# First loads on two queues, masks by half blocks, weight conversion from step 0, blocks stored after 9 steps, gates drawn from step 14: one change to an attention and two-layer expert kernel

## The chip, the core and the metric

The kernel runs on one core of one Trainium2 chip. The metric is the device time of one execution in microseconds (us). The kernel before takes 639.42 us in the median of three runs (639.33 to 639.66). The kernel computes in fp32. TensorE multiplies it as a high and a low part, so one product is three matmuls.

## The reference

B = 2, H = 8, S = 768, D = 64; `n_global` = 8, `n_local` = 96. The attention's output, 1536 tokens by 512, passes through two layers one after the other:

```python
scores = scale * q @ k.T + bias            # bias = -slope[h] * dist
keep = is_global | is_local                # first 8 keys, or the last 96 positions
a = softmax(where(keep, scores, -1e9)); x = a @ v          # -> 1536 x 512

h = (x @ w1) * (x @ w2) @ w3               # layer 1: 512 -> 1024 -> 1024
x = h @ w_out                              #          1024 -> 512
x = ((x @ w_a) * (x @ w_b)) @ w2_out       # layer 2: 512 -> 1536 -> 512
```

The inputs of the two layers' weights and the counts arrive as 64-bit words; a weight has to be converted on the chip into a high and a low fp32 part before TensorE can use it.

## The kernel before, in words

**Attention in steps.** A block is 128 queries of one batch (12 blocks); a unit is one pair of heads of a block, four units to a block, 48 units in all. The loop of `band_attention` runs over steps u. Each step puts work of several units on the engines' queues, in this order: the score matmuls of units u and u+1 on TensorE (even steps only, `sp`, L400), the exponentials of unit u-2 on ScalarE (L446), one stage of the mask generator, the transposes of unit u-5 on TensorE (`pt`, L470) with the copy out of PSUM on ScalarE (L472), the values of unit u-6 on TensorE (`pv`, L502). Then `feed` takes turns among the remaining pieces: the masked row maximum of unit u-1 on VectorE (L434), the normalisation of unit u-3 (VectorE L455, L457; GpSimd L459), the block stages that are due, and the conversion stages. Each engine runs its own queue in the order of writing, so an instruction that waits holds up everything written behind it on that engine.

**Block stages.** `block_stages` lists stage and lag in steps after the block's first unit: `store_x` copies a finished block's values into the high part `xh` (ScalarE, two instructions, L480) at lag 11, `store_x_low` subtracts for the low part `xl` (VectorE, two instructions, L486) at lag 12. Loads of keys and queries (`band_load`) have lag -6, loads of values lag 0.

**Weights.** The weights come in pieces of 512 KB (`raw`, loaded on SyncE's queue at L173). A piece passes four conversion stages, one per step: ScalarE L93 and L94 (`words`), VectorE L100, L104, L108 (`join`), ScalarE L112 (`upper`), VectorE L116 (`rest`). `feed` begins a new piece at steps 2, 5, 8 and so on, every fourth step from 20 on, and loads two pieces ahead. The result is a `w` tile.

**Gates.** After `feed`, each step draws from the generator `moe` (the "filler") while `spent` is below a budget: up to two draws of six TensorE matmuls each (`ab`, L639 to L641, 128 x 512 a matmul, or 128 x 256 for the half tiles at the start). A draw of a half tile adds 0.65 to `spent`, one of a full tile 1.3. A gate can only be drawn when its blocks are stored and its weights converted two steps before. A gate's first half tile needs the first two blocks, `xh` and `xl`. `fold` multiplies w3 and w_out on the chip, in draws of six matmuls too. `self.order` is the list in which gates and folds are drawn. When attention ends, the rest of the two layers follows without the step loop.

**The start.** `band_masks` builds the bias of each head from two numbers read from DRAM: `bias0` for a batch's first block (128 columns a head) and `bias` for the others (256 columns a head); ScalarE makes the even heads (L310), GpSimd the odd ones (L312). Keys and queries of block 0 (`kq0`) and the numbers (`ni`) are loaded on SyncE's queue at L785 and L787, before every engine reads the counts into registers (L793, L807).

Of the kernel before, what the change touches and what calls it, by code (L numbers as in the profile page):

```python
# [14 lines left out]
ALU = mybir.AluOpType  # L15

P = 128
# [14 lines left out]
class Emitter:  # L32
# [117 lines left out]
    def feed_start(self):  # L150
# [7 lines left out]
        self.order += [("gate", f, t, whole) for t in range(1, nt) for f in range(3)]  # L158
        self.order += gates(3) + folds(0, 2) + gates(4) + folds(2, 5) + gates(5) + folds(5, nf)
# [9 lines left out]
    def feed_load(self, n):  # L169
        while self.n_loaded < min(n, len(self.pieces)):  # L170
            _, src, shape = self.pieces[self.n_loaded]
            raw = self.unit("raw", shape, I32)
            self.nc.sync.dma_start(raw, src)  # L173
            self.raws.append(raw)
            self.n_loaded += 1

    def feed(self, others=(), force=False):


        turns = list(others)  # L180
        for piece in list(self.flight):
# [5 lines left out]
        if self.n_begun < len(self.pieces):  # L187
# [3 lines left out]
            pace = 3 if self.step < 20 else 4  # L191
            room = self.n_waiting < self.lead and not (self.patient and (self.step < 2 or (self.step - 2) % pace))
# [78 lines left out]
    def band_masks(self):  # L271
# [15 lines left out]

        nc.vector.tensor_scalar(out=gl[:, own], in0=gl[:, g], scalar1=self.ng, scalar2=None, op0=ALU.is_lt)
        nc.vector.tensor_scalar(out=loc, in0=rel, scalar1=0.0, scalar2=None, op0=ALU.is_ge)
        nc.vector.tensor_scalar(out=gl[:, g], in0=gl[:, own], scalar1=-far, scalar2=far, op0=ALU.mult, op1=ALU.add)  # L290
        nc.vector.scalar_tensor_tensor(out=loc, in0=rel, scalar=self.nl, in1=loc, op0=ALU.is_lt, op1=ALU.mult)
# [3 lines left out]
        nc.vector.tensor_tensor(out=near, in0=rel, in1=loc, op=ALU.mult)  # L295
        nc.vector.tensor_scalar(out=dist, in0=loc, scalar1=-far, scalar2=far, op0=ALU.mult, op1=ALU.add)
        yield

        nc.vector.tensor_scalar(out=rel[:, g], in0=loc[:, own], scalar1=-1.0, scalar2=1.0, op0=ALU.mult, op1=ALU.add)
        nc.vector.tensor_tensor(out=dist, in0=near, in1=dist, op=ALU.add)  # L300
        nc.vector.tensor_tensor(out=rel[:, g], in0=rel[:, g], in1=gl[:, g], op=ALU.mult)
        nc.vector.tensor_copy(out=dist0[:, MAX_GLOBAL:P], in_=dist[:, P + MAX_GLOBAL :])
        nc.vector.tensor_tensor(out=dist0[:, g], in0=near[:, own], in1=rel[:, g], op=ALU.add)
        nc.vector.tensor_copy(out=dist[:, g], in_=gl[:, g])


        for bias, d in ((self.bias0, dist0[:, :P]), (self.bias, dist)):
            for h in range(self.H):
                if h % 2 == 0:
                    nc.scalar.mul(bias[:, h, :], d, -self.slopes[h] / self.scale)  # L310
                else:
                    nc.gpsimd.tensor_scalar(  # L312
                        out=bias[:, h, :], in0=d, scalar1=-self.slopes[h] / self.scale, scalar2=1.0, op0=ALU.mult, op1=ALU.mult
                    )
                if h % 2 and (bias is self.bias or h == self.H - 1):
                    yield
# [192 lines left out]
    def band_attention(self, filler):  # L509
# [15 lines left out]
        next(masks)  # L525
        block_stages = (
            (C + 7, lambda t: self.store_x(t, self.pv[t])), (C + 8, lambda t: self.store_x_low(t, self.pv.pop(t))),
# [8 lines left out]
        for u in range(nu + C + 8):  # L536
# [13 lines left out]
            for _ in range(2):  # L550
                if spent < 0.7 * (u - 16):
# [224 lines left out]
def tile_kernel(ctx, tc, io):  # L776
# [7 lines left out]
    for r in range(2):  # L784
# [100 lines left out]
```

## Time and profile before

| what | us |
|---|---|
| median of three runs | 639.42 |
| the profiled execution's own time | 640.13 |
| its span in the trace | 638.3 |
| TensorE (PE) busy | 621.0 |
| VectorE (DVE) busy | 385.9 |
| ScalarE (ACT) busy | 301.0 |
| GpSimd (POOL) busy | 67.7 |

The span is the time from the first instruction to the last of the one profiled execution; its own time is measured around it and holds 1.83 us more. That execution took 0.71 us more than the median, so a time predicted for the median is the execution's own time, plus the change, less 0.71. The mean granted clock of TensorE over the span is 0.998 of full speed.

### The profile page before, as it was taken

What the parts mean: (1) busy time and instruction counts of PE and PEld (TensorE: products, weight loads), DVE (VectorE), ACT (ScalarE), POOL (GpSimd) and SP (SyncE); (2) the same over time, 40 slices, a digit from 0 to 9 for tenths busy, and PEclk for the clock granted to TensorE, in tenths of its full rate; (3) what the DMA queues carried; (4) which work ended last, traced back from release to release, by engine and by line L of the source; (5) the groups of instructions that cost most, each with busy time, mean ns of one, the idle gap of its engine ahead of it and who ended that gap; (6) DMA issues with size and microseconds to landing.
All of it is one profiled execution on the core that took longest, in us unless ns stands there. A gap on an engine that the chain in (4) does not pass through costs nothing.

```text
span 638.3 us, 8976 instructions
## 1 busy us (share of the span) xinstructions
PE 621.0 (97%) x3230; PEld 510.6 (80%) x3230; DVE 385.9 (60%) x874; ACT 301.0 (47%) x659; POOL 67.7 (11%) x118
## 2 busy tenths in 40 slices
PE   3989999999999999999999999999999999999996
PEld 3668888788888888888888888888888888888885
DVE  4888976369987576643314566556556556653343
ACT  4999887657666374723213453243243333331110
POOL 3656664300000000000000000000000000000000
PEclk9999999999999999999999999999999999999999
DMA  6999962343525142200005011111112112000004
GB/s 189 261 229 213 234 163 103 100 163 118 161 94 162 63 151 81 67 0 1 1 0 198 33 34 66 67 66 67 67 66 67 66 67 66 1 0 1 1 35 168
DMA packets 20148, 58.86 MB, mean 92 GB/s; under 512 B 2816, under 2 KB 3072, under 8 KB 20096
## 3 DMA queue, kind: packets, MB, share of 16 engines
q1 hardware_dynamic: 20096, 58.21, 31.2%
q8 instruction: 27, 0.44, 0.3%
q14 instruction: 25, 0.20, 0.1%
HBM read 55.05 MB, written 3.15 MB: 91 GB/s over the span
## 4 chain that ended last, share of the span: by engine, by line
PE 95%; ACT 1%; SPq 1%; DMA 1%; DVE 0%; issue 0%; POOL 0%; ACTq 0%; POOLq 0%
PE ab_band L639 18%; PE ab_band L641 17%; PE ab_band L640 17%; PE o_band L126 5%; PE o_band L127 5%; PE o_band L125 5%; PE pv_band L502 4%; PE y_band L127 3%; PE y_band L125 3%; PE y_band L126 3%; PE pt_band L470 3%; PE wfp_band L239 2%; PE wfp_band L237 2%; PE wfp_band L238 2%; PE sp_band L417 2%; PE sp_band L400 2%
## 5 line engine op out<-in xcount | busy, mean ns | idle before, releaser
L639 PE MATMUL ab_band<-y_band,w_band 128*128 128x512 f32 x288 | 112.0, 389 | 0.0
L640 PE MATMUL ab_band<-y_band,w_band 128*128 128x512 f32 x288 | 112.0, 389 | 0.0
L641 PE MATMUL ab_band<-y_band,w_band 128*128 128x512 f32 x288 | 112.0, 389 | 0.0
L646 ACT COPY b_band<-ab_band 128x512 f32<-128x512 f32 (+1 forms) x63 | 35.6, 567 | 157.2 <-PE ab_band L641 157.1
L639 PE MATMUL ab_band<-xh_band,w_band 128*128 128x512 f32 (+1 forms) x216 | 82.3, 381 | 0.0
L647 DVE TENSOR_TENSOR gg_band<-ab_band,b_band 128x512 f32<-128x512 f32 x36 | 24.9, 691 | 92.0 <-ACT b_band L646 92.0
L640 PE MATMUL ab_band<-xl_band,w_band 128*128 128x512 f32 (+1 forms) x216 | 79.0, 366 | 0.0
L641 PE MATMUL ab_band<-xh_band,w_band 128*128 128x512 f32 (+1 forms) x216 | 78.9, 365 | 0.0
L112 ACT CAST w_band<-g_band 128x512 fp32r<-128x512 f32 x76 | 47.3, 623 | 48.2 <-DVE g_band L108 47.2
L639 PEld LDWEIGHTS ab_band<-y_band,w_band 128*128 128x128 f32 x288 | 54.1, 188 | 11.3
L640 PEld LDWEIGHTS ab_band<-y_band,w_band 128*128 128x128 f32 x288 | 54.1, 188 | 11.2
L641 PEld LDWEIGHTS ab_band<-y_band,w_band 128*128 128x128 f32 x288 | 54.1, 188 | 11.1
L459 POOL TENSOR_SCALAR s_band<-s_band,z_band 128x256 f32<-128x256 f32 (+1 forms) x96 | 57.9, 616 | 42.9 <-DVE z_band L457 22.9
L108 DVE CUSTOM_DVE_ANT_0 g_band<-raw_band,g_band 128x1024 uint16<-128x1024 uint16 x76 | 53.0, 697 | 10.8 <-DVE g_band L104 0.5
L126 PE MATMUL o_band<-w_band,g_band 128*128 128x512 f32 (+1 forms) x146 | 56.4, 386 | 0.0
L127 PE MATMUL o_band<-w_band,g_band 128*128 128x512 f32 (+1 forms) x146 | 56.4, 386 | 0.0
L125 PE MATMUL o_band<-w_band,g_band 128*128 128x512 f32 (+1 forms) x146 | 56.4, 386 | 0.0
L104 DVE SCALAR_TENSOR_TENSOR g_band<-raw_band,g_band 128x512 int32<-128x512 int32 x76 | 52.5, 690 | 2.3
L116 DVE TENSOR_TENSOR w_band<-g_band,w_band 128x512 fp32r<-128x512 f32 x76 | 50.9, 686 | 2.9 <-ACT w_band L112 2.3
L93 ACT ACTIVATE g_band<-raw_band 128x512 f32<-128x512 f32 x76 | 50.8, 668 | 1.3 <-DMA raw_band<-in_moe_w_dram 1.3
L94 ACT ACTIVATE raw_band<-raw_band 128x512 int32<-128x512 uint32 x76 | 50.7, 666 | 0.0
L639 PEld LDWEIGHTS ab_band<-xh_band,w_band 128*128 128x128 f32 x216 | 40.5, 188 | 11.5 <-issue 4.6
(92 smaller groups left out, 1042.6 us busy)
## 6 DMA issues: line engine op xcount, KB each, us to landing
raw_band<-in_moe_w_dram SPq DMA_DIRECT2D x32, 512.0 KB, 4.0
raw_band<-in_moe_w_out_dram SPq DMA_DIRECT2D x20, 512.0 KB, 4.3
raw_band<-in_moe_w_a_dram SPq DMA_DIRECT2D x12, 512.0 KB, 3.7
raw_band<-in_moe_w_b_dram SPq DMA_DIRECT2D x12, 512.0 KB, 3.9
v_band<-in_v_dram SPq DMA_DIRECT2D x12, 256.0 KB, 7.7
kd_band<-in_kq_dram SPq DMA_DIRECT2D x12, 256.0 KB, 8.9
qd_band<-in_kq_dram SPq DMA_DIRECT2D x12, 256.0 KB, 9.1
out_dram<-acc_band SPq DMA_DIRECT2D x11, 256.0 KB, 2.0
```

Source lines behind the costliest of these rows:

```text
L93: nc.scalar.activation(out=g, in_=f32(high), func=AF.Copy, scale=WORD_SCALE)
L94: nc.scalar.activation(out=low, in_=low.bitcast(U32), func=AF.Copy, scale=2.0**-29)
L104: nc.vector.scalar_tensor_tensor(out=gi, in0=high, scalar=-0x80000000, in1=gi, op0=ALU.bitwise_and, op1=ALU.bitwise_or)
L108: nc.vector.tensor_tensor(out=gi, in0=gi, in1=low, op=ALU.add)
L116: nc.vector.tensor_tensor(out=lo, in0=g, in1=f32(hi), op=ALU.subtract)
L125: self.nc.tensor.matmul(out, wl, xh, start=(i == 0), stop=False)
L126: self.nc.tensor.matmul(out, wh, xl, start=False, stop=False)
L127: self.nc.tensor.matmul(out, wh, xh, start=False, stop=(i == n - 1))
L459: nc.gpsimd.tensor_scalar(out=s[:, j, lo:], in0=s[:, j, lo:], scalar1=z[:, j : j + 1], scalar2=1.0, op0=ALU.mult, op1=ALU.mult)
L639: nc.tensor.matmul(p, wl, xh, start=(c == 0), stop=False)
L640: nc.tensor.matmul(p, wh, xl, start=False, stop=False)
L641: nc.tensor.matmul(p, wh, xh, start=False, stop=(c == self.C - 1))
```

## The change

It does seven things, all in the attention phase and what prepares it. (1) The numbers, the second half of `kq0` and the first two raw weight pieces are loaded on ScalarE's queue; SyncE keeps the first half of `kq0`. (2) `band_masks` works on the upper 128 columns first, makes `bias0` from them in the same stage (ScalarE heads 0, 1, 4, 5; GpSimd the others), then the lower 128 columns, and the even heads of `bias` on VectorE. (3) Keys and queries of a block come in two DMAs of 256 KB in place of four of 128 KB. (4) Pieces are begun at steps 0, 2, 5, 8 and so on; in steps below 6 all attention turns of VectorE are written ahead of the conversion turns. (5) Blocks are stored two steps sooner (lags 9 and 10), and the loop is two steps shorter. (6) The budget is 0.85 (u - 13), less 0.15 for each step over 38, in place of 0.7 (u - 16), so draws begin at step 14 in place of 17. (7) In the list of draws the gates of f = 3 move ahead to the first group, and folds 2 to 7 come in one run after the gates of f = 5.

```diff
-        self.order += [("gate", f, t, whole) for t in range(1, nt) for f in range(3)]
-        self.order += gates(3) + folds(0, 2) + gates(4) + folds(2, 5) + gates(5) + folds(5, nf)
+        self.order += [("gate", 3, 0, whole)]
+        self.order += [("gate", f, t, whole) for t in range(1, nt) for f in range(4)]
+        self.order += gates(4) + folds(0, 2) + gates(5) + folds(2, 5) + folds(5, nf)
...
+        if self.patient and self.step < 6:
+            while turns:
+                for turn in list(turns):
+                    if next(turn, turns) is turns:
+                        turns.remove(turn)
...
-            pace = 3 if self.step < 20 else 4
-            room = self.n_waiting < self.lead and not (self.patient and (self.step < 2 or (self.step - 2) % pace))
+            due = self.step in (0, 2) or (self.step > 4 and (self.step - 2) % (3 if self.step < 20 else 4) == 0)
+            room = self.n_waiting < self.lead and (due or not self.patient)
...
+        local(slice(P, W))
+        first = dist0[:, own]
...
+            if h % 4 < 2:
+                nc.scalar.mul(self.bias0[:, h, :], dist0[:, :P], factor)
+            else:
+                nc.gpsimd.tensor_scalar(
...
+        local(slice(0, P))
...
+            engine = nc.vector if h % 2 == 0 else nc.gpsimd
+            engine.tensor_scalar(
+                out=self.bias[:, h, :], in0=dist, scalar1=factor, scalar2=1.0, op0=ALU.mult, op1=ALU.mult
+            )
...
-                for n in range(2):
-                    self.load_rows(self.kq[t][:, n], t, n)
+                for r in range(2):
+                    nc.sync.dma_start(
+                        self.kq[t][r * D : (r + 1) * D], self.io["kq"][b, i, :, :, r * self.C : (r + 1) * self.C]
+                    )
...
+        self.feed_load(self.ahead, self.nc.scalar)
         self.band_load(1)
-        self.feed_load(self.ahead)
...
-            (C + 7, lambda t: self.store_x(t, self.pv[t])), (C + 8, lambda t: self.store_x_low(t, self.pv.pop(t))),
+            (C + 5, lambda t: self.store_x(t, self.pv[t])), (C + 6, lambda t: self.store_x_low(t, self.pv.pop(t))),
...
-        for u in range(nu + C + 8):
+        for u in range(nu + C + 6):
...
-                if spent < 0.7 * (u - 16):
+                if spent < 0.85 * (u - 13) - 0.15 * max(u - 38, 0):
...
-    for r in range(2):
-        nc.sync.dma_start(kq0[r * D : (r + 1) * D], io["kq"][0, 0, :, :, r * H // 2 : (r + 1) * H // 2])
...
-        nc.sync.dma_start(ni, io["n"].unsqueeze(0).broadcast_to([P, 4]))
+        nc.scalar.dma_start(ni, io["n"].unsqueeze(0).broadcast_to([P, 4]))
+    for r, queue in enumerate((nc.sync, nc.scalar)):
+        queue.dma_start(kq0[r * D : (r + 1) * D], io["kq"][0, 0, :, :, r * H // 2 : (r + 1) * H // 2])
```

ScalarE (ACT), the start of its program before: the eight bias instructions, in between the exponentials of unit 0 (`s_band_276`), then the words of piece 0 (`raw_band_233`), the exponentials of units 1 to 3.

```order
L310 ACTIVATE bias_band_225<-dist_band_222 128x128 x4
L310 ACTIVATE bias_band_224<-dist_band_221 128x256 x2
L446 ACTIVATE s_band_276,z_band_286<-s_band_276,m_band_277 128x128 x2
L310 ACTIVATE bias_band_224<-dist_band_221 128x256
L93 ACTIVATE g_band_297<-raw_band_233 128x512
L94 ACTIVATE raw_band_233<-raw_band_233 128x512
L446 ACTIVATE s_band_300,z_band_306<-s_band_300,m_band_301 128x128 x2
L310 ACTIVATE bias_band_224<-dist_band_221 128x256
L446 ACTIVATE s_band_312,z_band_333<-s_band_312,m_band_313 128x128 x2
L112 CAST w_band_296<-g_band_297 128x512
L446 ACTIVATE s_band_340,z_band_349<-s_band_340,m_band_341 128x128 x2
L472 COPY pt_band_355<-pt_band_352 128x2x128
```

The same place of the changed kernel:

```order
L175 DMA raw_band_228<-in_moe_w_dram 128x1024
L175 DMA raw_band_230<-in_moe_w_dram 128x1024
L323 ACTIVATE bias_band_225<-dist_band_222 128x128 x4
L93 ACTIVATE g_band_277<-raw_band_228 128x512
L94 ACTIVATE raw_band_228<-raw_band_228 128x512
L471 ACTIVATE s_band_284,z_band_297<-s_band_284,m_band_285 128x128 x2
L112 CAST w_band_276<-g_band_277 128x512
L93 ACTIVATE g_band_310<-raw_band_230 128x512
L94 ACTIVATE raw_band_230<-raw_band_230 128x512
L471 ACTIVATE s_band_305,z_band_316<-s_band_305,m_band_306 128x128 x2
L471 ACTIVATE s_band_322,z_band_344<-s_band_322,m_band_323 128x128 x2
L112 CAST w_band_309<-g_band_310 128x512
```

The two raw loads stand on ScalarE's queue now, the even heads' `bias` is gone from it, and L93 and L94 of piece 0 stand ahead of the exponentials of unit 0, those of piece 1 ahead of unit 1.

TensorE (PE) before, around the first gate: the transposes of unit 11 and the values of unit 10 (step 16, rows 1 and 2), the transposes of unit 12 and the values of unit 11 (step 17, rows 3 and 4), then the first gate's half tile (`ab_band_772`). A name stands as out<-operands.

```order
L470 MATMUL pt_band_716<-ident,s_band_594 128x128 x4
L502 MATMUL pv_band_650<-pt_band_683,v_band_449 64x128 x4
L470 MATMUL pt_band_745<-ident,s_band_621 128x128 x4
L502 MATMUL pv_band_650<-pt_band_721,v_band_449 64x128 x4
L639 MATMUL ab_band_772<-xh_band_544,w_band_296 128x256
L640 MATMUL ab_band_772<-xl_band_545,w_band_296 128x256
L641 MATMUL ab_band_772<-xh_band_544,w_band_296 128x256
L639 MATMUL ab_band_772<-xh_band_544,w_band_296 128x256
```

The same place of the changed kernel, at step 14 (transposes of unit 9, values of unit 8, then the first gate):

```order
L495 MATMUL pt_band_652<-ident,s_band_534 128x128 x4
L527 MATMUL pv_band_659<-pt_band_622,v_band_458 64x128 x4
L663 MATMUL ab_band_685<-xh_band_489,w_band_276 128x256
L664 MATMUL ab_band_685<-xl_band_490,w_band_276 128x256
L665 MATMUL ab_band_685<-xh_band_489,w_band_276 128x256
L663 MATMUL ab_band_685<-xh_band_489,w_band_276 128x256
L664 MATMUL ab_band_685<-xl_band_490,w_band_276 128x256
L665 MATMUL ab_band_685<-xh_band_489,w_band_276 128x256
L663 MATMUL ab_band_685<-xh_band_491,w_band_276 128x256
L664 MATMUL ab_band_685<-xl_band_492,w_band_276 128x256
```

The gate's first six matmuls read `xh_band_489` and `xl_band_490` (heads 0 to 3 of the first two blocks), the next six `xh_band_491` and `xl_band_492` (heads 4 to 7).

VectorE (DVE) before, where block 1 is stored (step 16), one step ahead of the first gate: L434 is the maximum, L455 and L457 the normalisation, L486 the low part.

```order
L434 ISA s_band_731,m_band_732<-sp_band_631,bias_band_224 128x256
L434 ISA m_band_732 128x1
L455 TENSOR_SCALAR z_band_675<-z_band_675 128x2
L486 TENSOR_TENSOR xl_band_545<-pv_band_511,xh_band_544 128x2x128
L434 ISA s_band_731,m_band_732<-sp_band_631,bias_band_224 128x256
L434 ISA m_band_732 128x1
L457 RECIPROCAL z_band_675<-z_band_675 128x2
L486 TENSOR_TENSOR xl_band_547<-pv_band_511,xh_band_546 128x2x128
```

The same place of the changed kernel (step 14, the step of the first gate):

```order
L459 ISA s_band_671,m_band_672<-sp_band_576,bias_band_224 128x256
L459 ISA m_band_672 128x1
L480 TENSOR_SCALAR z_band_614<-z_band_614 128x2
L511 TENSOR_TENSOR xl_band_490<-pv_band_526,xh_band_489 128x2x128
L116 TENSOR_TENSOR w_band_560<-g_band_561,w_band_560 128x512
L459 ISA s_band_671,m_band_672<-sp_band_576,bias_band_224 128x256
L459 ISA m_band_672 128x1
L482 RECIPROCAL z_band_614<-z_band_614 128x2
L511 TENSOR_TENSOR xl_band_492<-pv_band_526,xh_band_491 128x2x128
```

The first low part stands behind one maximum as before; between the two there is now also the last conversion stage (L116) of the fifth piece, and all of it stands in the step in which the first gate is drawn.

## Rows read from the trace of the kernel before

**Rows 1.** The page: TensorE's busy time; the chain that ended last, by engine.
```profile
PE 621.0 (97%) x3230; PEld 510.6 (80%) x3230; DVE 385.9 (60%) x874; ACT 301.0 (47%) x659; POOL 67.7 (11%) x118
...
PE 95%; ACT 1%; SPq 1%; DMA 1%; DVE 0%; issue 0%; POOL 0%; ACTq 0%; POOLq 0%
```

**Rows 2.** Windows: us, then PE, PEld, DVE, ACT, POOL busy, clock, DMA, GB/s.
```profile
10.00:20.00 10.00, 6.93 (x42) 4.79 (x40) 6.97 (x34) 8.75 (x33) 6.14 (x13) 1.00 1.04 306
41.70:638.30 596.60, 591.53 (x2982) 489.02 (x2978) 355.87 (x732) 268.97 (x558) 46.06 (x75) 1.00 0.28 83
```

**Rows 3.** Waits of TensorE: total us, times, longest us.
```profile
PE pv_band L502 <- ACT pt_band L472: 2.6, 3, 1.6
```

**Rows 4.** Chain of waits in the first 43 us: start, us, what.
```profile
2.74 1.34 SPq L793
...
5.41 0.51 SPq L327
...
7.87 4.81 DMA raw_band<-in_moe_w_dram
...
16.30 2.01 PE sp_band L400 x16
...
25.18 1.09 PE sp_band L400 x16
```

**Rows 5.** Timeline of TensorE around the first gate: start, us, what.
```profile
35.41 0.67 PE L502 MATMUL pv_band<-pt_band,v_band 128*64 128x128 f32 x8
36.01 0.66 PE L470 MATMUL pt_band<-ident,s_band 128*128 128x128 f32 x4
36.59 0.66 PE L502 MATMUL pv_band<-pt_band,v_band 128*64 128x128 f32 x8
...
41.78 0.39 PE L639 MATMUL ab_band<-xh_band,w_band 128*128 128x256 f32 x1
...
43.39 0.49 PE L400 MATMUL sp_band<-kq_band,kq_band 64*128 64x128 f32 x4
```

**Rows 6.** Timeline of SyncE's DMA issues, first row.
```profile
0.74 1.32 SPq L785 DMA_DIRECT2D kq<-in_kq_dram  x2
```

**Rows 7.** DMA issues in the first 14 us: last number, us to landing.
```profile
kq<-in_kq_dram SPq DMA_DIRECT2D x2, 256.0 KB, 3.9
```

**Rows 8.** All raw loads of the first 30 us: issue to landing.
```profile
DMA to landing us min/median/max: 4.8/6.9/7.7
```

**Rows 9.** Timeline of ScalarE, 12 to 20 us.
```profile
12.71 0.66 ACT L93 ACTIVATE g_band<-raw_band 128x512 f32<-128x512 f32 x1 [1.25 <-DMA raw_band<-in_moe_w_dram]
...
13.83 0.39 ACT L446 ACTIVATE s_band<-s_band,m_band 128x128 f32<-128x128 f32 x1
...
14.60 0.40 ACT L310 ACTIVATE bias_band<-dist_band 128x256 bf16<-128x256 f32 x1
...
17.21 0.67 ACT L93 ACTIVATE g_band<-raw_band 128x512 f32<-128x512 f32 x1
...
18.34 0.49 ACT L446 ACTIVATE s_band<-s_band,m_band 128x256 f32<-128x256 f32 x1
```

**Rows 10.** Timeline of ScalarE, 26 to 37 us.
```profile
27.84 0.62 ACT L112 CAST w_band<-g_band 128x512 fp32r<-128x512 f32 x1
28.36 0.51 ACT L446 ACTIVATE s_band<-s_band,m_band 128x256 f32<-128x256 f32 x1
...
29.36 0.57 ACT L472 COPY pt_band<-pt_band 128x512 f32<-128x512 f32 x1
29.82 0.64 ACT L480 CAST xh_band<-pv_band 128x256 fp32r<-128x256 f32 x2
30.35 0.72 ACT L93 ACTIVATE g_band<-raw_band 128x512 f32<-128x512 f32 x1
```

**Rows 11.** Timeline of VectorE, 30 to 39.5 us.
```profile
35.10 0.69 DVE L116 TENSOR_TENSOR w_band<-g_band,w_band 128x512 fp32r<-128x512 f32 x1 [0.16 <-ACT w_band L112]
35.71 0.41 DVE L434 CUSTOM_DVE_ANT_0 s_band<-sp_band,bias_band 128x256 f32<-128x256 f32 x1
```

More of the change, by code (lines that the diff above doesn't have):

```diff
@@ L167, in feed_start, with feed_load @@
         self.place = {key: i for i, (key, _) in enumerate(self.jobs)}
-    def feed_load(self, n):
+    def feed_load(self, n, queue=None):
+        queue = queue or self.nc.sync
         while self.n_loaded < min(n, len(self.pieces)):
@@ L172, in feed_load @@
             raw = self.unit("raw", shape, I32)
-            self.nc.sync.dma_start(raw, src)
+            queue.dma_start(raw, src)
             self.raws.append(raw)
@@ L294, in band_masks @@
         )
-        nc.vector.tensor_tensor(out=near, in0=rel, in1=loc, op=ALU.mult)
-        nc.vector.tensor_scalar(out=dist, in0=loc, scalar1=-far, scalar2=far, op0=ALU.mult, op1=ALU.add)
+        local(slice(P, W))
+        first = dist0[:, own]
+        nc.vector.tensor_scalar(out=first, in0=loc[:, own], scalar1=-1.0, scalar2=1.0, op0=ALU.mult, op1=ALU.add)
+        nc.vector.tensor_tensor(out=dist0[:, :P], in0=near[:, P:], in1=dist[:, P:], op=ALU.add)
+        nc.vector.tensor_tensor(out=first, in0=first, in1=gl[:, g], op=ALU.mult)
@@ L297, in band_masks @@
+        nc.vector.tensor_tensor(out=dist0[:, g], in0=near[:, own], in1=first, op=ALU.add)
+        for h in range(self.H):
+            factor = -self.slopes[h] / self.scale
+            if h % 4 < 2:
+                nc.scalar.mul(self.bias0[:, h, :], dist0[:, :P], factor)
+            else:
+                nc.gpsimd.tensor_scalar(
+                    out=self.bias0[:, h, :], in0=dist0[:, :P], scalar1=factor, scalar2=1.0, op0=ALU.mult, op1=ALU.mult
+                )
         yield
-        nc.vector.tensor_scalar(out=rel[:, g], in0=loc[:, own], scalar1=-1.0, scalar2=1.0, op0=ALU.mult, op1=ALU.add)
+        local(slice(0, P))
@@ L300, in band_masks @@
         nc.vector.tensor_tensor(out=dist, in0=near, in1=dist, op=ALU.add)
-        nc.vector.tensor_tensor(out=rel[:, g], in0=rel[:, g], in1=gl[:, g], op=ALU.mult)
-        nc.vector.tensor_copy(out=dist0[:, MAX_GLOBAL:P], in_=dist[:, P + MAX_GLOBAL :])
-        nc.vector.tensor_tensor(out=dist0[:, g], in0=near[:, own], in1=rel[:, g], op=ALU.add)
         nc.vector.tensor_copy(out=dist[:, g], in_=gl[:, g])
[L307 to L316, printed above, removed]
+        for h in range(self.H):
+            factor = -self.slopes[h] / self.scale
+            engine = nc.vector if h % 2 == 0 else nc.gpsimd
+            engine.tensor_scalar(
+                out=self.bias[:, h, :], in0=dist, scalar1=factor, scalar2=1.0, op0=ALU.mult, op1=ALU.mult
+            )
+            if h % 2:
+                yield
@@ L334, in band_load @@
                 self.kq[t] = self.unit("kq", [P, 2, self.C, P])
[L335 to L336 removed]
+                for r in range(2):
+                    nc.sync.dma_start(
+                        self.kq[t][r * D : (r + 1) * D], self.io["kq"][b, i, :, :, r * self.C : (r + 1) * self.C]
+                    )
         else:
```

9 lines of the change are left out of this document (6 added, 3 removed).

## The prediction, as it was made before the changed kernel ran

> **What bounds the kernel now.** I read the page first, then windows, then the waits and the start of the chain, then single engines there. TensorE is busy for 621.0 of 638.3 us and holds 95% of the chain [rows 1]; the reader should look for the few microseconds in which it isn't. They lie in the first 42: from 41.70 to the end it is busy for 591.53 of 596.60 us, at full granted clock, while VectorE and ScalarE have two fifths and more of that stretch free [rows 2]. So the end is the moment at which TensorE becomes continuous, plus the work that is then left. That moment is the first gate, at 41.78 [rows 5]: before it TensorE still waits for the copies of transposes on ScalarE, 2.6 us in three waits [rows 3]. And what sets the pace up to there is ScalarE, which waits for the first raw piece (1.25 us, until 12.71) and then runs without a break, words, exponentials and copies in one queue [rows 9, 10].
>
> The chain shows why the first piece comes then [rows 4]: SyncE issues the loads of block 0, reads the counts (from 2.74), issues the next block's loads from 5.41 on, and the raw piece at 7.87; that lands 4.81 us later.
>
> **The change, term by term.** I make the sum for the moment at which TensorE becomes continuous.
>
> *A. Gates from step 14.* The gates' slot of step 14 opens when the values of unit 8 end, at 36.01 [rows 5]. Before, 5.77 us pass from there to the first gate. In them lie three transposes (0.58 each, 36.01 to 36.59), three values (0.60 each, 35.41 to 36.01) and one set of scores (1.09, [rows 4]), together 4.63. That work isn't saved, it only comes behind the gates. The rest, 5.77 - 4.63 = 1.14, is waiting that the gates now fill. **Gain 1.1.**
>
> *B. The whole front comes sooner.* New head: the words of piece 0 stand in front of the exponentials of unit 0 on ScalarE, so everything there begins when the first raw piece lands. Its DMA is the third on ScalarE's queue. Two issues take 0.74 to 2.06 on SyncE [rows 6]; reading the counts took SyncE 5.41 - 2.74 = 2.67 [rows 4]; so it goes out at about 4.7 in place of 7.87. For its flight the trace gives 3.9 us for 256 KB at the very start [rows 7] and 4.8 to 7.7 for raw pieces, median 6.9 [rows 8]. The first of its queue and only just behind block 0, it is nearest to the two low rows: 8.6 to 9.5, I take **9.0**; the far bound is 4.7 + 7.7 = 12.4. I cost the masks at nothing: before, ScalarE was through with unit 0's and stood idle 1.25 us for the piece [rows 9], and now less mask work stands ahead of it on VectorE and ScalarE, and the numbers are the first load of a queue. If they are late all the same, it is unit 0's exponentials that wait, and these stand behind the words, whose 1.13 us cover as much.
>
> From there to the exponentials of unit 12 ScalarE has, in its new order: five pairs of words at 1.13 (17.21 to 18.34), four exponential pairs of 128 columns at 0.77 (13.83 to 14.60) [rows 9]; five high parts (L112) at 0.52, eight pairs of 256 columns at 1.00, five copies of 512 at 0.46, four copies of 256 at half of that, two stores at 0.53 [rows 10]. That is 5.65 + 3.08 + 2.60 + 8.00 + 2.30 + 0.92 + 1.06 = 23.6 us. To it come waits: behind the words stand the three joining passes on VectorE before L112 can run, and only one exponential pair fills them for pieces 0 and 1, an estimate of 0.9 each from the VectorE passes of 0.6 to 0.7 (the row of L116 is one of them [rows 11]), and 0.3 for a store that waits for its values. So exponentials of unit 12 start at 9.0 + 23.6 + 2.1 = 34.7. The values of unit 8 need the copy of unit 8, which stands ahead of one store (0.53) and one high part (0.52): it ends at 33.7, and the values, which began at 35.41 before, begin there. **Gain 1.7.** The slot of step 14 opens at 34.3.
>
> *C. A new wait in that slot.* The first gate's second half reads the second low part of block 1. VectorE makes it in the same step, behind the conversion's last stage (L116), a maximum and a reciprocal. L116 waits for L112, which ends as unit 12's exponentials start (34.7), plus 0.16; it takes 0.61 (35.10 to 35.71), the maximum 0.4 and the low part, of the same 128 x 256, about 0.4 [rows 11]. That is 36.3. The first half of the gate is done at 34.3 + 0.8 (twelve such matmuls took 41.78 to 43.39 [rows 5]), so TensorE waits 1.2 in front of the second. Queued behind are all its attention steps. **Loss 1.2.** Bounds: nothing, if VectorE has those passes done by then, or 2, if the maximum waits too.
>
> *At nothing:* larger key loads, the lower columns of the masks, one more conversion and the even heads' bias on VectorE (its share of that early stretch is 6.97 of 10 us [rows 2]), gates of f = 3 ahead of the folds (the same matmuls in another order; weights convert in time as long as VectorE keeps the room that it shows there, 355.87 of 596.60), and the shorter loop.
>
> Sum: 1.1 + 1.7 - 1.2 = 1.6 us sooner. The profiled execution took 640.13 for its span of 638.3, which is 0.71 above the median; so the time is 638.5 by that execution and **637.8** by the median.
>
> **Rivals.** The scale first: 0.2% is 1.3 us, about what a measurement of this kernel can tell from no change.
>
> *No difference: the raw piece shares the engines.* The sum hangs on the landing: each microsecond later than 9.0 is a microsecond less. Beside the raw piece go the second raw piece and block 1's keys and queries, 512 KB each. At the 306 GB/s of the saturated stretch [rows 2] these 1.5 MB take 5.1 us, and if all three end together the piece lands at 4.7 + 5.1 = 9.8 at best and, with the 0.7 that the first two issues took on SyncE each [rows 6] as a start, at 10.5: then the gain is 0.1 and the time **639.3**. For it: the DMA engines stand at 1.04 of their share there. Against it: the first raw piece took 4.81 while another raw piece and the keys flew beside it. The Trainium skill ("DMA: Bandwidth & Descriptors", section "Issuing engines are not separate DMA queues") says that DMAs started by different engines run on the same 16 engines and interleave, so that a second issuing engine only saves the time of issuing. By that rule this rival is the whole of the second queue's effect: 3.2 us of issue, and no faster flight. The trace of before, with one issuing engine, cannot show it.
>
> *Slower: the raw piece takes as long as the longest before.* 7.7 us [rows 8] from 4.7 is 12.4; the front is then 1.7 us later than with no gain at all, and A less C gives nothing back: **641.2**. It decides from a landing at about 11.9 on, where the sum is -1.3. For it: SyncE sends block 1's keys, values and a third raw piece in the same stretch, which it did later before. Against it: the raw loads with the long flights were issued later, behind full queues; this one has none ahead of it.
>
> *Faster still: no new wait.* If VectorE runs ahead of ScalarE in step 14, C is nothing and the time **636.6**. Against it: L116 can't run before L112, which stands directly ahead of the exponentials of unit 12.
>
> *TensorE stays at its lower rate longer.* The same 16 score matmuls take 2.01 us at 16.30 and 1.09 at 25.18 [rows 4]: by that TensorE ran at the lower of its levels (1.2 of 2.4 GHz) up to some point between, though the windows print a granted clock of 1.00 there [rows 2]; it had waited for much of the time before. If the front comes 3 us sooner but with more holes, the lower rate may last as long as before; since ScalarE sets the pace there, I give that 0.3 us and no chance of its own.
>
> **How the numbers follow.** My forecast (landing up to 9.3, or later with a smaller wait) has 0.40, no new wait 0.12, sharing within 0.2% 0.33, slower 0.15. Faster by over 0.2% takes the first two, 0.52. The range runs from 635.5 (landing at 8.6, no wait, and a microsecond of the lower rate gained) to 640.4, a landing at 11.6, near the end of the sharing case; what lies outside is most of the slower case and the far end of the best.
>
> **What would show it.** First L93 at 9.0; exponentials of unit 12 at 34.7; first gate at 34.3, then a wait of about 1.2 us for VectorE's L511 in front of an L664; no wait of TensorE for ScalarE's copies after 37. Wrong would be: L93 later than 10.5; TensorE waiting after the first gate for copies or weights, which would mean that ScalarE or the conversions still set the pace with the steeper budget; or waits for weights at the folds that now stand in one run.

## The result, and the profile after

The changed kernel takes 645.05 us in the median of four runs (643.51 to 645.95) against 639.38: a ratio of 1.0079 with a 95% interval of 1.0066 to 1.0092. The medians differ by 5.7 us, the ratio corresponds to 5.1 (4.2 to 5.9): it is slower, where 1.6 us less had been forecast. Its profiled execution has a span of 643.4 us, 5.1 more than before.

The page of the changed kernel: busy times, and the granted clock in 40 slices (tenths of full speed). The first line answers to [rows 1].

```profile
PE 622.1 (97%) x3230; PEld 510.7 (79%) x3230; DVE 387.8 (60%) x882; ACT 301.4 (47%) x655; POOL 69.2 (11%) x118
...
PEclk9999998999999999999999999999999999999999
```

TensorE's work is nearly the same (622.1 us busy against 621.0), so the 5.1 us are time in which it waits, or runs at a lower rate: one slice of the clock, the seventh, from 97 to 113 us, stands at 8 tenths. The waits of TensorE in the changed kernel (total us, times, longest us):

```profile
PE sp_band L425 <- DMA kq<-in_kq_dram: 5.8, 2, 5.6
...
PE pv_band L527 <- ACT pt_band L497: 2.4, 3, 1.1
PE ab_band L664 <- DVE xl_band L511: 1.8, 1, 1.8
PE pt_band L495 <- POOL s_band L484: 1.0, 1, 1.0
PE pt_band L495 <- ACT g_band L93: 0.5, 1, 0.5
```

The first two lines belong to the start, before the first gate. The last three are new, and all lie behind 70 us. Where they cost is seen in windows of the changed kernel (columns as in [rows 2]):

```profile
42.00:70.00 28.00, 28.00 (x274) 23.67 (x274) 23.34 (x84) 24.49 (x72) 14.77 (x20) 1.00 0.94 216
70.00:95.00 25.00, 23.48 (x181) 18.87 (x180) 20.95 (x82) 19.20 (x62) 15.70 (x23) 1.00 0.70 180
95.00:112.00 17.00, 15.15 (x109) 11.59 (x107) 9.32 (x35) 11.50 (x31) 6.96 (x12) 0.90 0.11 29
112.00:140.00 28.00, 27.86 (x214) 21.65 (x213) 12.49 (x61) 17.50 (x54) 10.24 (x20) 1.00 0.40 129
105.00:110.00 5.00, 5.00 (x34) 3.91 (x33) 1.33 (x9) 2.66 (x7) 2.86 (x5) 0.70 0.00 0
```

and in one of the kernel before:

```profile
70.00:112.00 42.00, 41.82 (x352) 34.70 (x348) 31.33 (x130) 32.66 (x103) 22.74 (x38) 1.00 0.62 157
```

Up to 70 us nothing is lost. Between 70 and 112 TensorE is not busy for 1.52 + 1.85 = 3.37 us (0.18 before), and from 105 to 110 its granted clock is 0.70. What the low clock costs is seen in two equal groups of eight score matmuls in the chain of the changed kernel, 0.95 us at 94 and 1.81 at 107:

```profile
94.21 0.95 PE sp_band L442 x8
...
106.59 1.81 PE sp_band L442 x8
```

The start, on the other hand, came nearly as forecast. TensorE around the first gate, to be read against [rows 5]:

```profile
32.47 0.67 PE L527 MATMUL pv_band<-pt_band,v_band 128*64 128x128 f32 x8 [1.08 <-ACT pt_band L497]
...
34.16 0.66 PE L495 MATMUL pt_band<-ident,s_band 128*128 128x128 f32 x4
34.74 0.67 PE L527 MATMUL pv_band<-pt_band,v_band 128*64 128x128 f32 x8
35.34 0.39 PE L663 MATMUL ab_band<-xh_band,w_band 128*128 128x256 f32 x1
...
36.16 0.28 PE L663 MATMUL ab_band<-xh_band,w_band 128*128 128x256 f32 x1
36.46 0.39 PE L664 MATMUL ab_band<-xl_band,w_band 128*128 128x256 f32 x1
```

ScalarE at the first words and at the exponentials of unit 12:

```profile
8.60 0.66 ACT L93 ACTIVATE g_band<-raw_band 128x512 f32<-128x512 f32 x1 [0.43 <-DMA raw_band<-in_moe_w_dram]
...
34.78 0.57 ACT L471 ACTIVATE s_band<-s_band,m_band 128x256 f32<-128x256 f32 x1
```

The first words run at 8.60 (forecast 9.0), the exponentials of unit 12 at 34.78 (34.7), the first gate at 35.34 (34.3), with 0.3 us lost in it between 36.16 and 36.46 (1.2). The first gate is 6.44 us sooner than before; 4.63 of these are work that moved behind it, 0.2 to 0.3 the new wait, so at 42 us the kernel is 1.5 to 1.6 us ahead. It then loses 6.6.

Why TensorE waits is read on VectorE. Its timeline in the changed kernel (L671 is the product that ends a gate, L395 and L398 the low parts of the next block's keys and queries, L511 the low part of a stored block):

```profile
75.97 0.43 DVE L671 TENSOR_TENSOR g_band<-ab_band,b_band 128x256 f32<-128x256 f32 x1 [2.74 <-ACT b_band L670]
...
76.85 1.22 DVE L395 TENSOR_TENSOR ks_band<-kd_band,ks_band 64x1024 fp32r<-64x1024 f32 x1
...
79.13 1.21 DVE L398 TENSOR_TENSOR qb_band<-qd_band,qa_band 128x1024 fp32r<-128x1024 f32 x1
...
98.43 0.69 DVE L671 TENSOR_TENSOR g_band<-ab_band,b_band 128x512 f32<-128x512 f32 x1 [4.35 <-ACT b_band L670]
...
99.58 1.22 DVE L395 TENSOR_TENSOR ks_band<-kd_band,ks_band 64x1024 fp32r<-64x1024 f32 x1
...
101.26 1.21 DVE L398 TENSOR_TENSOR qb_band<-qd_band,qa_band 128x1024 fp32r<-128x1024 f32 x1
...
102.79 0.42 DVE L511 TENSOR_TENSOR xl_band<-pv_band,xh_band 128x256 fp32r<-128x256 f32 x1
```

Twice VectorE stands at a gate's product, 2.74 us up to 75.97 and 4.35 us up to 98.43, because TensorE has not finished that gate and ScalarE has not copied it (L670). Behind it, after one maximum, come L395 and L398 with 1.2 us each, and what TensorE needs next stands behind those: at 103 the first gate of the second tile waits for the low part that L511 writes at 102.79.

```profile
103.27 0.50 PE L664 MATMUL ab_band<-xl_band,w_band 128*128 128x512 f32 x1 [1.84 <-DVE xl_band L511]
```

### The profile page after: what moved, and what is told of

The parts are those of the page before. It is cut to its first block, busy times and chain, and to the rows that moved or that the text cites. A ratio compares the mean times of both kernels' runs of the same rounds, so it can differ in the third digit from the quotient of the medians.

```text
span 643.4 us, 8956 instructions
## 1 busy us (share of the span) xinstructions
PE 622.1 (97%) x3230; PEld 510.7 (79%) x3230; DVE 387.8 (60%) x882; ACT 301.4 (47%) x655; POOL 69.2 (11%) x118
## 4 chain that ended last, share of the span: by engine, by line
PE 92%; DVE 3%; ACT 3%; issue 1%; DVEq 0%; POOL 0%; ACTq 0%; POOLq 0%
PE ab_band L663 18%; PE ab_band L664 17%; PE ab_band L665 17%; PE o_band L127 5%; PE o_band L125 5%; PE o_band L126 5%; PE y_band L126 3%; PE y_band L125 3%; PE y_band L127 3%; PE pv_band L527 3%; PE pt_band L495 3%; PE wfp_band L246 2%; PE wfp_band L245 2%; PE wfp_band L247 2%; PE sp_band L442 2%
## 5 line engine op out<-in xcount | busy, mean ns | idle before, releaser
L670 ACT COPY b_band<-ab_band 128x512 f32<-128x512 f32 (+1 forms) x63 | 35.6, 567 | 155.9 <-PE ab_band L665 155.8
L671 DVE TENSOR_TENSOR gg_band<-ab_band,b_band 128x512 f32<-128x512 f32 x36 | 24.9, 691 | 92.2 <-ACT b_band L670 92.2
L484 POOL TENSOR_SCALAR s_band<-s_band,z_band 128x256 f32<-128x256 f32 (+1 forms) x96 | 58.9, 624 | 56.1 <-DVE z_band L482 39.2
L116 DVE TENSOR_TENSOR w_band<-g_band,w_band 128x512 fp32r<-128x512 f32 x76 | 52.4, 705 | 3.0 <-ACT w_band L112 2.4
L93 ACT ACTIVATE g_band<-raw_band 128x512 f32<-128x512 f32 x76 | 51.0, 671 | 0.4 <-DMA raw_band<-in_moe_w_dram 0.4
L94 ACT ACTIVATE raw_band<-raw_band 128x512 int32<-128x512 uint32 x76 | 51.1, 673 | 0.0
```

The source lines that it names most:

```text
L93: nc.scalar.activation(out=g, in_=f32(high), func=AF.Copy, scale=WORD_SCALE)
L94: nc.scalar.activation(out=low, in_=low.bitcast(U32), func=AF.Copy, scale=2.0**-29)
L116: nc.vector.tensor_tensor(out=lo, in0=g, in1=f32(hi), op=ALU.subtract)
L484: nc.gpsimd.tensor_scalar(out=s[:, j, lo:], in0=s[:, j, lo:], scalar1=z[:, j : j + 1], scalar2=1.0, op0=ALU.mult, op1=ALU.mult)
```

## The experiments

All times are medians; the ratio is to runs of the kernel before on the same chip (639.4 to 639.8 there); "idle" is the time in which TensorE is not busy from 70 to 112 us of the profiled execution.

| run | us | ratio to before, 95% interval | idle, us |
|---|---|---|---|
| changed kernel | 645.05 | 1.0066 to 1.0092 | 3.37 |
| e1 start alone | 640.37 | 1.0000 to 1.0022 | 0.18 |
| e2 flatter budget | 642.98 | 1.0028 to 1.0057 | 1.16 |
| e3 gates held one step | 644.77 | 1.0069 to 1.0099 | 3.39 |
| e4 all products later | 641.11 | 1.0015 to 1.0035 | 0.88 |
| e5 split one step sooner | 639.11 | 0.9984 to 1.0003 | 0.00 |
| e6 old store lags | 643.42 | 1.0038 to 1.0064 | 1.15 |
| e7 old order of gates | 641.98 | 1.0022 to 1.0042 | 0.96 |
| e8 e4 and e5 | 640.13 | 0.9992 to 1.0016 | 0.27 |
| e9 two products later | 641.16 | 1.0012 to 1.0030 | 0.85 |
| e10 all but these two | 645.68 | 1.0081 to 1.0112 | 3.31 |
| e11 e5, keys first | 639.94 | 1.0002 to 1.0033 | 0.00 |
| e12 e8, keys first | 640.10 | 1.0000 to 1.0019 | 0.14 |
| e13 draws alone | 644.65 | 1.0066 to 1.0104 | 3.95 |
| e14 e5 without the start | 639.54 | 0.9992 to 1.0018 | 0.10 |

### e1: the start alone

```diff
-                if spent < 0.85 * (u - 13) - 0.15 * max(u - 38, 0):
+                if spent < 0.7 * (u - 16):
```
with the store lags, the loop and the order of gates of before.

> The new start alone (first loads on two queues, masks by half blocks, conversion from step 0) with the budget, the order of gates and the store lags of before. Theory M (the loss is made after 70 us by the drawing of gates, and the start gains 1.5): first L93 at about 8.6, no TensorE wait between 70 and 130 us, granted clock 1.00 there, time 637.5 to 638.2. Rival F (the start is at fault, since earlier conversions fill VectorE later on): TensorE waits of some us after 70 us and a time of 642 or more.

Theory M was right on the place (no new wait behind 70 us), wrong on the time: 640.37, no gain. In its profile:

```profile
32.43 0.89 PE L526 MATMUL pv_band<-pt_band,v_band 128*64 128x128 f32 x8 [1.62 <-ACT pt_band L496]
33.25 0.80 PE L424 MATMUL sp_band<-kq_band,kq_band 64*128 64x128 f32 x4
...
42.25 0.38 PE L662 MATMUL ab_band<-xh_band,w_band 128*128 128x256 f32 x1
```

TensorE waits 1.62 us for the copy of unit 7 and runs the next scores at the lower rate (0.80 for the first four, 0.49 at the full one), and its first gate is at 42.25, no sooner than the 41.78 of before [rows 5].

### e2, e3: a flatter budget, and gates held one step

```diff
-                if spent < 0.85 * (u - 13) - 0.15 * max(u - 38, 0):
+                if spent < 0.7 * (u - 13):
```

> The changed kernel with a budget of 0.7 (u - 13): draws still begin at step 14, but gates of the second tile are reached at step 43 in place of 38. Theory M: the wait of 1.84 us for the low part at 103 us and the lower clock behind it are gone, VectorE keeps up, 638 to 639. Rival F: still 642 or more. Rival O (the order of gates or the earlier storing is at fault, at any slope): waits of TensorE for VectorE's results around 80 to 105 us stay, 641 or more.

```diff
-            while self.stored * P < tg * TG + at.stop or ...
+            while self.stored * P < tg * TG + at.stop or (self.patient and tg and self.step <= self.stored_at) or ...
```

> The changed kernel, but a gate of the second or third tile is drawn at the earliest one step after its last block was stored. Theory M1 (the loss is mostly the one wait for the low part in step 38, 1.84 us, and the lower clock behind it, 1.9 us): that wait is gone, granted clock 1.00 around 105 us, time 641 to 641.5. Rival M2 (VectorE itself is late there, the wait only moves to the next thing that it makes): 643.5 to 645 as before.

e3 lets a gate of the second or third tile be drawn at the earliest one step after its last block was stored (the dots stand for the rest of the line). The flatter budget takes away 2.1 us of the 5.7, so a steep budget is not all of it; with the gates held, the wait for the low part is gone, but TensorE waits 1.9 us at one set of transposes for L484 instead, and the time stays. The second is what M2 said: VectorE is late, and whatever it makes next is waited for.

### e4: the product of a gate one draw later

```diff
-                if c % 2 and not (w is pair[-1] and c == self.C - 1):
+                if c % 2 and (self.patient or not (w is pair[-1] and c == self.C - 1)):
                     yield 1.3 * (at.stop - at.start) / TG
             ps.append(p)
...
-            yield 1.3 * (at.stop - at.start) / TG
+            if not self.deferred:
+                yield 1.3 * (at.stop - at.start) / TG
```

The draw now ends ahead of the copy and the product, and these are written at the start of the next draw.

> The changed kernel with the copy and the product of a finished gate written one draw later, behind the maxima of the next step, so that VectorE does not stand at the product while TensorE still works at that gate. Theory Q (VectorE's waits in its queue, 2.74 us at 76 and 4.35 us at 98, make its block work late, and TensorE waits for it): these waits shrink below 1 us, the waits of TensorE at 80, 91 and 103 us too, 638.5 to 640.5. Rival: VectorE is simply short of time there, 643 to 645; or the gate's banks come free later and TensorE waits for them, over 645.

641.11: 3.9 us of the loss are gone with the same matmuls in the same order, a little less than theory Q said. So TensorE's waits come from VectorE's waits in its own queue.

### e5 to e7: which part of the change brings it

e5 moves the split, and with it the loads, of the second batch's blocks:

```diff
-            (0, self.band_load_v), (C - 1, self.band_global), (-3, self.band_low), (-4, self.band_high), (-6, self.band_load),
+            (0, self.band_load_v), (C - 1, self.band_global), (-4, self.band_low), (-5, self.band_high),
+            (-8, lambda t: None if self.whole(t) else self.band_load(t)), (-6, lambda t: self.band_load(t) if self.whole(t) else None),
```

> The changed kernel with the split of keys and queries (high and low part) one step sooner for the second batch's blocks, at lags -5 and -4 in place of -4 and -3, and their loads at lag -8. With the stores of before the two heavy VectorE stages of a block fell in steps 0 and 1 of every four, light steps behind; with the earlier stores they fall in steps 1 and 2, ahead of the conversion's joining passes in step 3. Theory L (this bunching makes VectorE late, and TensorE waits for maxima and normalised rows at 80 to 105 us): the stages fall in steps 0 and 2 now, the waits for L484 and for the low part shrink by half or more, 640 to 642. Rival Q (only the standing at a gate's product matters): 643.5 to 645.5.

e6 undoes the earlier storing:

```diff
-            (C + 5, lambda t: self.store_x(t, self.pv[t])), (C + 6, lambda t: self.store_x_low(t, self.pv.pop(t))),
+            (C + 7, lambda t: self.store_x(t, self.pv[t])), (C + 8, lambda t: self.store_x_low(t, self.pv.pop(t))),
...
-                if spent < 0.85 * (u - 13) - 0.15 * max(u - 38, 0):
+                if spent < 0.85 * (u - 16) - 0.15 * max(u - 41, 0):
```

> The changed kernel with the store lags of before (11 and 12), and the same budget slope and order three steps later (draws from step 17). Theory L (the earlier storing is what makes VectorE late): no waits of TensorE for L484 between 60 and 110 us, 639 to 640.5. Rival S (the steep budget makes the gates catch up with storing): the waits stay, in particular a wait for the low part at the first gate of the second tile, drawn at step 41, one step behind its storing; 642 to 645.

e7 takes the budget of e2 and the `self.order` of before:

> The changed kernel with the order of gates of before and a budget of 0.7 (u - 13): the first tile has three gates, done at step 35, and steps 36 and 37 draw nothing, since the second tile's blocks are not stored. Beside the run with the same budget and the new order (643.0) it shows the order alone. If the order is at fault: 640 to 641. If the earlier storing is at fault: 643 or, with the two empty steps, up to 645.

e5 gives the whole loss back, more than either theory said: 639.11, TensorE never idle from 70 to 112 us.

```profile
70.00:112.00 42.00, 42.00 (x335) 34.11 (x334) 35.72 (x135) 34.95 (x106) 26.42 (x40) 1.00 0.51 135
```

But e6 speaks against theory L as I had put it: with the old lags the loss stays at 4 us. Nor is it rival S, whose wait for the low part at step 41 did not occur. e7, at 641.98 between its two cases, shows that the order alone isn't it either. What e6 shares with the changed kernel is seen on its VectorE:

```profile
74.53 0.42 DVE L671 TENSOR_TENSOR g_band<-ab_band,b_band 128x256 f32<-128x256 f32 x1 [2.54 <-ACT b_band L670]
...
75.41 1.22 DVE L395 TENSOR_TENSOR ks_band<-kd_band,ks_band 64x1024 fp32r<-64x1024 f32 x1
```

It stands 2.54 us at a product, and the split of keys (L395) follows. TensorE's idle time there is 1.15 us in e6, so this is only a part of its 4 us. In the program the split is written in steps 21, 25, 29 and so on (lag -3), and the gates end, in the changed kernel, in steps 16, 19, 22, 25, 28, 31 and 36; in e6 in 19, 22, 25, 28, 31, 34, 39; before, in 19, 23, 27, 30, 34, 38. A gate that ends in a step divisible by four has its product right ahead of the split; the changed kernel has two of them among the split steps (28 and 36), e6 one (28), the kernel before none. By the same count e2 and e7 have two early ones (20 and 24): in e2 VectorE stands at these products for 2.21 us at 54.13 and 1.61 at 64.49, with L395 at 55.00 and 65.23, and TensorE waits 0.69 us at 69. In e5 the split stands ahead of such a product, and VectorE works through it while TensorE still multiplies; at the first of the two products (L672) there is no wait any more, and at the second, at 97.22, it is 1.58 us, with the split already done:

```profile
73.78 1.34 DVE L395 TENSOR_TENSOR ks_band<-kd_band,ks_band 64x1024 fp32r<-64x1024 f32 x1
...
75.44 1.21 DVE L398 TENSOR_TENSOR qb_band<-qd_band,qa_band 128x1024 fp32r<-128x1024 f32 x1
76.74 0.42 DVE L672 TENSOR_TENSOR g_band<-ab_band,b_band 128x256 f32<-128x256 f32 x1
```

e5 moves the loads of keys too. That these come sooner is not what helps: among ScalarE's waits in the changed kernel from 42 to 128 us there is none for a load.

### e8: both cures

The edits of e4 and e5 together.

> Both cures together: the product of a gate written one draw later, and the split of keys and queries one step sooner. If standing at the product (Q) and bunching (L) are two causes, this takes away both: no wait of TensorE over 0.5 us behind 42 us, and the 1.6 us that the changed kernel is ahead at 42 us are kept: 637.5 to 639. If they are one cause, 641 as with the deferred product alone.

640.13: nothing beyond e5. Waits of TensorE over 0.5 us behind 42 us are gone, as said, but in its profiled execution TensorE reached the full rate late (four score matmuls take 0.80 us at 21.19 and 26.11, as in e9 in the last section), and the time is no better.

### e9, e10: the two products, and all the others

```diff
+    def late_product(self):
+        return self.patient and self.step in (28, 36)      # e10: not in
...
-                if c % 2 and not (w is pair[-1] and c == self.C - 1):
+                last = w is pair[-1] and c == self.C - 1
+                if c % 2 and (not last or self.late_product()):
+                    late = last
                     yield 1.3 * (at.stop - at.start) / TG
```

> The changed kernel with the copy and product written one draw later for two gates alone, those that end in steps 28 and 36. Theory P (it is the phase: a gate that ends in a step divisible by four makes VectorE stand at its product directly ahead of the step that splits the next block's keys and queries, 2.4 us of VectorE, so that the wait cannot be made up): these two products are the whole effect, the waits of TensorE at 80, 91 and 103 us go, 640 to 641.5, as with all products deferred. Rival Q (every wait at a product adds up): little is gained, 643 to 645.

> The opposite: all products of the attention phase one draw later, except those of the two gates that end in steps 28 and 36. Theory P: the waits at 80, 91 and 103 us stay, 643.5 to 645.5. Rival Q: most of the gain of the run with all products deferred, 641 to 642.5.

This pair, on one chip, decides it. VectorE's longest group of waits from 70 to 110 us, none of them at a product, and TensorE's window in e9:

```profile
DVE ks_band L395 <- ACT ks_band L383: 4.5, 3, 1.8
```

```profile
70.00:112.00 42.00, 41.15 (x327) 33.13 (x328) 36.09 (x137) 35.11 (x108) 25.53 (x39) 1.00 0.48 127
```

and in e10, where the group at the product (L677) is back:

```profile
DVE g_band L677 <- ACT b_band L676: 8.6, 4, 4.4
```

```profile
70.00:112.00 42.00, 38.69 (x282) 30.62 (x282) 29.39 (x116) 30.11 (x91) 20.57 (x33) 0.96 0.43 111
```

Two products of 0.4 and 0.7 us, written one draw later, take the time from 645.05 to 641.16, the same as all of them together (641.11). All the others written later, and these two left, give 645.68. Rival Q falls also by the sum of VectorE's waits at products from 42 to 128 us, here in the changed kernel and in the kernel before:

```profile
DVE g_band L671 <- ACT b_band L670: 15.9, 6, 4.3
```

```profile
DVE g_band L647 <- ACT b_band L646: 10.7, 7, 3.7
```

The kernel before stands at products for 10.7 us, and its TensorE is idle for 0.18 us from 70 to 112; the VectorE of e2, 2.1 us faster than the changed kernel, stands there for 12.2. Of the two theories P is left: it matters what stands behind the waiting product.

### e11, e12: keys ahead of the second piece

```diff
-        self.feed_load(self.ahead, self.nc.scalar)
+        self.feed_load(1, self.nc.scalar)
         self.band_load(1)
+        self.feed_load(self.ahead)
```

> The version with the split of keys and queries one step sooner, and only the first raw piece on ScalarE's queue, the second on SyncE's behind block 1's keys and queries. If these land sooner by the second raw piece's share (1 to 2 us before 13.3), TensorE begins the second scores at about 11.5 and reaches its full rate sooner: up to 1.2 us less than with the split alone, 638 to 639. If the second piece's words come late by it, no gain: 639 to 640.

> The same with every product of the attention phase one draw later. If the 0.6 us waits that are left at gates' ends (at 55 and 69 us) are worth taking away: 637.5 to 638.5; if the later writing itself costs what it saves: 638.5 to 640.

Neither gains: 639.94 and 640.10, though the keys do land sooner: the last wait of the second scores for them ends at 11.49 in e11, at 13.30 in the changed kernel.

```profile
11.49 0.58 PE L425 MATMUL sp_band<-kq,kq_band 64*128 64x128 f32 x1 [1.01 <-DMA kq_band<-in_kq_dram]
```

```profile
13.30 0.58 PE L425 MATMUL sp_band<-kq,kq_band 64*128 64x128 f32 x1 [2.17 <-DMA kq_band<-in_kq_dram]
```

The profiled execution of e12 has the shortest span of all profiled ones, 637.4, but the times of e12 go from 639.05 to 642.26, and no interval lies below 1. I found no version that beats the kernel before beyond its interval; e5 is nearest.

### e13, e14: the draws without the start

The kernel before with the lags, the budget and the order of the changed one (e13), and with the edit of e5 besides (e14).

> The kernel before with only the draws of the changed one: stores at lags 9 and 10, budget from step 14, the new order of gates; loads, masks and the first conversions as before. Theory: the start is worth little, since the values of unit 8 were held by TensorE's own work and not by ScalarE's copy, and the two waits ahead of blocks' splitting come from the draws alone: waits for L459 or for the low part at about 80 and 103 us as in the changed kernel, 643 to 645.5. Rival: the start is worth 1.7 us, so without it 646 to 647.

> The same with keys and queries split one step sooner. Theory: no long wait is left behind 42 us, and the start of before serves as well as the new one: 638.5 to 639.8. Rival: without the new start 1 to 1.7 us more than with it (639.1 measured there), 640 to 641.

644.65 and 639.54: with and without the new start the same, in either company (645.05 and 639.11). The draws alone make the loss, with the same waits of TensorE, here from 42 to 140 us of e13:

```profile
PE ab_band L641 <- DVE xl_band L487: 2.4, 1, 2.4
PE pt_band L471 <- POOL s_band L460: 1.0, 1, 1.0
```

## Why the prediction was wrong

**The step that failed** is the premise of the sum, "the end is the moment at which TensorE becomes continuous, plus the work that is then left", and with it the last item, "at nothing", which left VectorE out because it "keeps the room that it shows there, 355.87 of 596.60". TensorE became continuous 1.5 us sooner, as forecast, and did not stay so: from 70 to 112 us it is idle for 3.37 us (0.18 before). The signs of being wrong named waits for copies or weights; behind 70 us TensorE waited mostly for low parts and normalised rows, which VectorE, or GpSimd behind it, made late.

The room was a mean over 600 us, and not even the load nearby tells the cases apart: from 70 to 95 us VectorE is busy for 20.95 of 25 us in the changed kernel, 20.52 before, and 23.73 in e5, which loses nothing. What counts there is whether VectorE is ahead of TensorE when the four-step cycle brings its two long passes. Gates that end in another step move the place at which VectorE must wait for TensorE. I had priced the moved draws on TensorE alone, and had not followed the last instructions of a gate, the copy and the product, into the queues of ScalarE and VectorE. The gate of f = 3 that change (7) moves ahead, "the same matmuls in another order", is the one that ends in step 36 and holds VectorE for 4.35 us. The list of gates' ends could have been had from the order of the program. e9 and e10 show that two such products are 3.9 us of the 5.7, e13 that the loss needs nothing of the new start. e5 shows that nothing is lost when the split stands ahead of them.

**Term A** (1.1) and **term B** (1.7), less **term C** (1.2): the sum at 42 us was right, by two sizes that were off and cancel. B measured 0.67, not 1.7: the values of unit 8 were not held by ScalarE's copy of unit 8 (it ended where I said) but by TensorE's own run from the values of unit 7, at 32.47 where it had been 33.14 before, through scores and transposes. For the same reason the slot opened a microsecond later, when the low part was nearly ready, and C was 0.3. So the size of the lead was right by luck. That ScalarE runs "without a break" before the first gate was misread too: in the kernel before it waits 1.07 us for TensorE's transposes, up to 23.52. The low end of the range was summed wrongly: 637.8 less 0.4, 1.2 and 1.0 is 635.2, not 635.5; nothing hangs on it.

**The landing.** 8.60, by 0.4 sooner than taken. The rival of shared engines (10.5) did not occur for the first piece: it was issued at 4.64 and used 3.96 us later (4.84 before). Half of block 0's keys, issued on the same queue at 1.16, was still in flight then. Other loads came later: those of block 0 took 4.7 and 5.4 us to land on the two queues, 3.9 before [rows 7], and TensorE's first scores began at 5.62 (4.60 before).

```profile
kq<-in_kq_dram SPq DMA_DIRECT2D x1, 256.0 KB, 4.7
kq<-in_kq_dram ACTq DMA_DIRECT2D x1, 256.0 KB, 5.4
```

For block 1's keys e11 shows the sharing: without the second raw piece beside them they land 1.8 us sooner. The interleaving that the Trainium skill states ("DMA: Bandwidth & Descriptors", section "Issuing engines are not separate DMA queues") agrees with these rows for the start as a whole.

**The slower rival** named the wrong mechanism (a late landing, 641.2); the sign had 0.15, its cause none of it. And the 1.5 us ahead at 42 us do not last in the median: of e1 against before, e13 against the changed kernel and e14 against e5 none shows a gain of the start, to within some 0.2%. The single execution of the changed kernel reached TensorE's full rate early, others with the same first steps did not (last section). How much each course weighs in the medians is open, since only the profiled execution of a kernel shows it.

**What stays open.** Waits (3.2 us more than before from 70 to 112 us) and the low clock (0.70 for 5 us, by estimate 1.5) make some 5 us of the 6.6 lost behind 70 us; the rest is spread over small gaps that I could not place. That the low clock at 105 us follows from the wait of 1.84 us just before is not settled: e10 and e13, with waits of 1.8 and 2.4 us there, have a granted clock of 0.96 from 70 to 112 us, e5 and e9, without them, 1.00, but e3 has 1.00 too, with a wait of 1.9 us at another instruction. No run changed such a wait's length alone. e4 and e9 are still 1.3 and 1.7 us slower than the kernel before, with 0.9 us of idle TensorE from 70 to 112; e5 takes this away too, and no run shows why. Nor does each product ahead of a split cost: in e4 VectorE stands at one for 1.97 us at 53.82, L395 follows at 54.69, and TensorE does not wait until 70.

## What to carry to other kernels

When work is drawn into a loop by a budget, follow the last instruction of each unit, the one that reads the result on another engine, into that engine's queue: it stands there until the producer is done, and what is long and needed soon is better written ahead of it than behind. A mean of an engine's load over the kernel says nothing on that; the cycle of the loop, with its heavy and light steps, does. When a change moves many things, undo one phase relation (here a lag by one step) before undoing the parts.

## What the runs showed of the hardware that I had not expected

When TensorE rises to its full rate is not fixed by the program. e9 and the changed kernel have the same program up to step 28 and start their scores within 0.1 us of each other, yet the 16 score matmuls at 21 and those at 24 to 26 us run at different rates. The changed kernel:

```profile
21.01 0.49 PE L425 MATMUL sp_band<-kq_band,kq_band 64*128 64x128 f32 x4 [0.33 <-DVE kq_band L409]
...
24.14 0.49 PE L425 MATMUL sp_band<-kq_band,kq_band 64*128 64x128 f32 x4
```

and e9:

```profile
21.09 0.80 PE L425 MATMUL sp_band<-kq_band,kq_band 64*128 64x128 f32 x4 [0.19 <-DVE kq_band L409]
...
26.02 0.80 PE L425 MATMUL sp_band<-kq_band,kq_band 64*128 64x128 f32 x4
```

It is not the chip either: e10, on the chip of e9 and with the same program up to step 16, has

```profile
21.12 0.49 PE L425 MATMUL sp_band<-kq_band,kq_band 64*128 64x128 f32 x4 [0.45 <-DVE kq_band L409]
```

Four of them take 0.49 us at the upper level (2.4 GHz) and 0.80 at the lower (1.2 GHz); e9 is at the lower one still at 26 us. The windows of e9 print a granted clock of 1.00 there all the same; those of e2, whose first steps are the same too, show 0.73 and 0.50:

```profile
20.00:22.00 2.00, 1.32 (x12) 1.08 (x14) 1.86 (x10) 2.00 (x8) 1.22 (x2) 0.73 1.05 299
22.00:24.00 2.00, 2.00 (x16) 1.45 (x16) 2.00 (x10) 1.08 (x5) 1.70 (x3) 0.50 1.05 208
```

TensorE had waited off and on in all of them before that. In e9 the first gate came at 37.36, 2 us later than in the changed kernel; two sets of scores at the lower rate, 2.0 in place of 1.09 us each, are 1.8 of it. That is more than any part of the change was forecast to be worth.
